# The two passes over the F tiles of a feed-forward layer, in the other order: six tiles first, eight second

## The chip, the cores and the metric

The kernel runs on one core of a Trainium2 chip. Its time is the device time of one execution in microseconds (us), the median over runs. One further execution was recorded by the hardware profiler, and all rows below are from that one. TensorE (PE in the rows) multiplies matrices and writes PSUM; PEld is its loading of weights, which overlaps the multiplying. VectorE (DVE), ScalarE (ACT) and GpSimd (POOL) do the elementwise work; SyncE (SP) issues the DMA transfers, one after the other in the order of its queue. Each engine works through its own queue in order, and a semaphore holds it where an operand isn't there yet.

## The reference

```python
xn = _layernorm(x)                          # x: 8192 tokens of 448
s  = irfft(mlp(rfft(xn)))                   # Fourier transform over the tokens, a two-layer
                                            # complex MLP in 4 blocks of 112, soft threshold
g  = silu((gelu(xn @ w_gate) * (xn @ w_up)) @ w_down)      # D = 448, F = 1792
out = x + s * g
```

All is float32; the kernel splits each operand into a high and a low fp16 half and adds three products.

## The kernel before, in words

The tokens go in 16 chunks of 512, and F in 14 tiles of 128. The weights of all 14 F tiles do not fit at once, so the feed-forward layer (`ffn`) goes over the F tiles in two passes, `PF`: pass 0 over tiles 0 to 7, pass 1 over tiles 8 to 13. Pass 0 leaves its part of the down product in DRAM (`prt`); pass 1 reads it back (`pt`), adds its own and goes on with silu.

Within a pass a chunk (`chunk`) handles its F tiles in pairs. One pair is a `unit`: seven products of half-size operands (`a1` to `a7`, `product`) in the manner of Strassen and Winograd, on combined weights (`wt[f]`, slots 8 to 15, made by `gu_comb`) and on transposed combinations of the tokens, which come by two transposing DMA loads per chunk: `xta` (products 1, 5, 6, 7) and `xtb` (2, 3, 4). Both rings have one buffer: the load of the next chunk's `xta` can start when the last unit of a chunk has done its products on `xta`, that of `xtb` after the unit's last product `a4`. After the units come the down products (`down`), four groups of tokens by three matmuls for each F tile; they cover these loads.

Chunks 0 and 1 of pass 0 go another way (`plain`): 22 matmuls of 512 columns for each F tile, on plain transposes, because the combinations aren't made yet. At their end the down products of both chunks are done together. The down inputs of the second chunk (its h, fp16 halves) and its transposed tokens lie in slots of `wt` that the combined weights of tiles 2 to 7 need later, so `gu_comb` waits on the events `spare`, set tile by tile while the second chunk's down product runs.

While pass 0 runs, phase 1 goes on beside it: `chunk1(c)` for c = 2 to 17 loads the tokens of chunk c (16 and 17 are chunks 0 and 1 again, for pass 1), normalises them, writes the combinations to DRAM (`xts`), and does the first stage of the Fourier transform (`stage1`: 12 matmuls, results `ysb`). Beside that the weights of pass 1's tiles are prepared (`gu_block(b, 1)`), written to DRAM (`wsp`, `dsp`) and fetched at the end of pass 0 (`far_pair`, `far_down`). Phase 2 (`zero`, `group`: the middle of the transform and its MLP) and phase 3 (`tiles3`: the inverse transform and the output) go beside the rest of the feed-forward layer.

The order of instructions on all engines is fixed when the program is built. A planner (`Pace`) keeps an estimated clock for each engine and lets the tasks issue in the order of their estimated times; some have due times written by hand: `chunk1(c)` starts at `T1 + (c - 2) * DT`, with T1 = 84 and DT = 40. On the chip these due times do nothing but decide the order. PSUM has two banks for each of `bx`, `by`, `bd`, `bf`; the two `by` banks are freed by VectorE's additions `u<-by,u` and `v<-by,v`.

Of the kernel before, what the change touches and what calls it, by code (L numbers as in the profile page):

```python
# [26 lines left out]
BLK = ((0, 1), (1, 1)) + tuple((f, 2) for f in range(2, 14, 2))  # L27
NBK = len(BLK)

PF = ((0, 8), (8, 6))  # L30
PB = ((0, 5), (5, 8))
K1, K2 = 256, 192


# [286 lines left out]
def afno_geglu_kernel(ctx, tc, x, gu, wd, mlp, b1, b2, c_m, c_mt, c_small, out):  # L321
# [22 lines left out]
    def ring(pool, shape, dt, name, bufs):  # L344
        return Ring(pace, pool, shape, dt, name, bufs)
# [28 lines left out]
    mhalf = cp.tile([128, CH], F32, name="mhalf")  # L374


    wt = [cp.tile([128, 2, 16, 128], F16, name=f"wt{f}") for f in range(PF[0][1])]
    dw = [cp.tile([128, PF[0][1], D], F16, name=f"dw{i}") for i in range(2)]
    ms = cp.tile([128, 32], F32, name="ms")
    cB = [fb[:, 0:1], fb[:, 1:2]]  # L380
    cF = ms[:, 24:25]
# [22 lines left out]
    EV = {}  # L404

    def ev(*key):
        return EV.setdefault(key, Event())
# [20 lines left out]
    WO = ring(wp, [128, 2, 14, 128], F16, "wo", 1)  # L428
    XTA = ring(fp, [128, XA // 128, 256], F16, "xta", 1)
    XTB = ring(fp, [128, (XW - XA) // 128, 256], F16, "xtb", 1)  # L430
    HT = ring(fp, [128, PF[0][1], 2, 512], F16, "h", 1)
    U1 = ring(fp, [128, 512], F32, "u1", 2)
    U5 = ring(fp, [128, 512], F32, "u5", 1)
    V1 = ring(fp, [128, 512], F32, "v1", 1)
# [153 lines left out]
            if c + 1 < NG + PL:  # L588
                yield ev("phase", c)

    T1, DT = 84.0, 40.0


    def gu_loads(fs, again):
# [83 lines left out]
    def gu_comb(f, t, d):  # L678

        c = yield from CB.get()  # L680
        S.activation(t[:, 4:9], t[:, 4:9], AF.Copy, scale=scale(f, 2))
        yield
        b22 = t[:, 2:10:7]
        for o, p, q in ((c[:, 0:2], t[:, 0:2], t[:, 4:6]), (c[:, 2:4], b22, c[:, 0:2]), (c[:, 4:6], b22, t[:, 0:2]),
                        (c[:, 6], t[:, 6], c[:, 2]), (c[:, 7], t[:, 7], t[:, 3]), (t[:, 8], t[:, 10], t[:, 8])):
            B.tensor_sub(o, p, q)
            yield
        B.tensor_add(c[:, 7], c[:, 7], t[:, 8])
        yield
        WS.put(t)  # L690
        yield
        if 2 <= f < PF[0][1]:
            yield ev("spare", f - 2 if f < 6 else f)
        S.activation(d[:, 0], c, AF.Copy, scale=scale(f, 0))
        yield
        V.scalar_tensor_tensor(d[:, 1], c, scale(f, 0), d[:, 0], op0=ALU.mult, op1=ALU.subtract)
        CB.put(c)
        yield
        done("comb", f)

    def down_weights(p):
        fp0, nf = PF[p]
        if p == 0:

            parts, rings, kept = [(0, 4), (4, 2), (6, 2)], {0: WO, 4: XTB, 6: CB}, {}
        else:
            parts = [(fp0 + k, min(3, nf - k)) for k in range(0, nf, 3)]

        def load(f, n):
            if p == 0 and f in kept:  # L710
                return kept[f]
            if p == 0:
                t = yield from rings[f].get()
                w = t.rearrange("p s v c -> p (s v c)") if len(t.shape) == 4 else t.rearrange("p a b -> p (a b)")
                w = w if f == 6 else w.bitcast(F32)
            else:
                t = w = yield from WS.get()
            v = w[:, 0:n * D].rearrange("p (t d) -> p t d", t=n)
            if p == 0:
                kept[f] = t, v  # L720
            Q.dma_start(v, wd[128 * f:128 * (f + n), :].rearrange("(t p) d -> p t d", p=128))
            yield
            return t, v

        def most(f, n):
            t, v = yield from load(f, n)
            for i in range(n):
                V.tensor_reduce(dmx[:, f + i:f + i + 1], v[:, i], axis=AXIS.X, op=ALU.max, apply_absolute_value=True)
                yield
            if p == 1:  # L730
                WS.put(t)

        def split(f, n):
            t, v = yield from load(f, n)
            if p == 1:
                do = yield from WO.get()
                dv = do.rearrange("p s v c -> p (s v c)")[:, 0:2 * n * D].rearrange("p (s t c) -> p s t c", s=2, t=n)
            for i in range(n):
                d = [w[:, f + i] for w in dw] if p == 0 else [dv[:, s, i] for s in range(2)]
                sc = fd[:, 2, block(f + i):block(f + i) + 1]  # L740
                S.activation(d[0], v[:, i], AF.Copy, scale=sc)
                yield
                V.scalar_tensor_tensor(d[1], v[:, i], sc, d[0], op0=ALU.mult, op1=ALU.subtract)
                if p == 0:
                    done("dw", f + i)
                yield
            (WS if p == 1 else rings[f]).put(t)
            if p == 1:
                Q.dma_start(dsp[:, :, f - fp0:f - fp0 + n, :], dv)
                WO.put(do)  # L750

        for e in [pace.spawn(most(*q)) for q in parts]:
            yield e
        for b in range(*PB[p]):
            yield ev("scales", b)
        mx, ed, eguv = (fd[:, i] for i in range(3))
        bs, fs = slice(*PB[p]), slice(fp0, fp0 + nf)
        dm = dmx[:, 14 + fp0:14 + fp0 + nf]
        yield from largest(dm, dmx[:, fs], 2.0 ** -30)
        pow2(dm, dm)  # L760
        for b in range(*PB[p]):
            f, n = BLK[b]
            V.tensor_tensor(ed[:, b:b + 1], dmx[:, 14 + f:15 + f], dmx[:, 13 + f + n:14 + f + n], op=ALU.max)
        V.tensor_tensor(eguv[:, bs], fe[:, 0, bs], fe[:, 1, bs], op=ALU.mult)
        V.tensor_tensor(ed[:, bs], eguv[:, bs], ed[:, bs], op=ALU.mult)
        ED, inv = fb[:, 2:3], fb[:, 3:4]
        V.tensor_reduce(ED, ed[:, bs], axis=AXIS.X, op=ALU.max)
        V.reciprocal(inv, ED)
        V.tensor_scalar(eguv[:, bs], eguv[:, bs], inv, 2.0 ** 14, op0=ALU.mult, op1=ALU.mult)
        V.tensor_scalar(cB[p], ED, 2.0 ** -11, None, op0=ALU.mult)  # L770
        yield
        for q in parts:
            e = pace.spawn(split(*q))
            if p == 1:
                yield e
        yield e
# [104 lines left out]
    def xt_load(i, kind, first):  # L881
        yield ev("xts", i)
        R, cols = (XTA, slice(0, XA)) if kind == "a" else (XTB, slice(XA, XW))
        t = EV[f"xt{kind}", first, i] = yield from R.get()
        Q.dma_start_transpose(t, xts[i][:, cols])
        yield
        done("xt", kind, first, i)
# [194 lines left out]
    def ended(p, i, a, b, R):  # L1082
# [33 lines left out]
        Q.dma_start(ov[:, CH * i + a, :], th)  # L1116
        TH.put(th)

    def ffn():
        h = yield from HT.get()  # L1120
        yield ev("xp", 0, 0)

        def spare(n):
            g, k = (2 + n // 2, n % 2)
            return wt[g][:, k, 12:16].rearrange("p k c -> p (k c)")

        def h1(f, s):
            if f < 6:
                return wt[2 + f][:, s, 8:12].rearrange("p k c -> p (k c)")
            return wt[f][:, s, 12:16].rearrange("p k c -> p (k c)")  # L1130

        EV["hT", 0], EV["hT", 1] = (lambda f, s: h[:, f, s]), h1
        EV["xT", 1] = [spare(t) for t in range(7)]
        pace.set(ev("second"))
        nf = PF[0][1]

        n = [0, 0]
        while n[1] < nf:
            if n[0] < nf and (ev("w", n[0]).done or n[1] == n[0] or not all(ev("xp", 1, a).done for a in range(CH))):
                c = 0  # L1140
            else:
                c = 1
            yield from plain(c, n[c])
            yield pe()
            n[c] += 1
            if (c, n[c]) == (0, nf):
                XTA.put(state["xta"])
                pace.spawn(xt_load(PL, "a", 0))
        pace.spawn(xt_load(PL, "b", 0))
        for a in range(CH):  # L1150
            yield from down(0, 0, a, 0, nf, EV["hT", 0])
            yield pe()
        HT.put(h)
        rings = (BD, BD, BX, BX)
        for a in range(CH):
            state["d", a] = yield from rings[a].get()
        for f in range(nf):
            for a in range(CH):
                yield from down(0, 1, a, f, f + 1, h1, rings[a])
            pace.then(lambda f=f: done("spare", f))  # L1160
            yield pe()
        for p in range(2):
            for i in range(NG):
                if p or i >= PL:
                    yield from chunk(p, i)

    def chunk(p, i):
# [33 lines left out]
        XTB.put(xb)  # L1201
        if (p, i) == (0, NG - 1):
            pace.spawn(far_pair(nf // 2 - 1))
        if nxt:
            pace.spawn(xt_load(nxt[1], "b", nxt[0]))
        yield pe()
# [356 lines left out]
    def token(c, a, xs):  # L1563
# [18 lines left out]
        if c == 0:  # L1582
            parts = [(state["plain"][:, :, cols], pt)]
        else:
            yield ev("second")
            parts = [(wt[2 + k][:, 0:2 if k < 3 else 1, 12 + POS[a]], pt[:, 2 * k:min(2 * k + 2, 7)]) for k in range(4)]
        for dst, src in parts:
            if a in (0, 2):
                S.copy(dst, src)
# [126 lines left out]
```

## Time and profile before

| | |
|---|---|
| time, median of 3 runs | 1863.16 us (1861.73 to 1868.89) |
| the profiled execution | 1866.04 us, of which the span of its instructions is 1864.3 us |
| TensorE busy | 1816.7 us, 97% of the span |
| VectorE, ScalarE, GpSimd busy | 67%, 53%, 15% |
| tokens of chunk 0 and 1 (plain), to the last plain matmul | 119.0 us |
| first unit of pass 0 | 159.5 us |
| first matmul of phase 3 | 1500.2 us |

A share of busy time is a mean over the span. TensorE's idle time, and whether it runs at full clock, is to be read by stages.

### The profile page before, as it was taken

What the parts mean: (1) busy time and instruction counts of PE and PEld (TensorE: products, weight loads), DVE (VectorE), ACT (ScalarE), POOL (GpSimd) and SP (SyncE); (2) the same over time, 40 slices, a digit from 0 to 9 for tenths busy, and PEclk for the clock granted to TensorE, in tenths of its full rate; (3) what the DMA queues carried; (4) which work ended last, traced back from release to release, by engine and by line L of the source; (5) the groups of instructions that cost most, each with busy time, mean ns of one, the idle gap of its engine ahead of it and who ended that gap; (6) DMA issues with size and microseconds to landing.
All of it is one profiled execution on the core that took longest, in us unless ns stands there. A gap on an engine that the chain in (4) does not pass through costs nothing. (4 is left out here: it accounts for less than half of the span.)

```text
span 1864.3 us, 35733 instructions
## 1 busy us (share of the span) xinstructions
PE 1816.7 (97%) x14605; PEld 1331.8 (71%) x14605; DVE 1245.0 (67%) x2040; ACT 981.3 (53%) x1683; POOL 287.5 (15%) x365
## 2 busy tenths in 40 slices
PE   6999999999999999999999999999999999999998
PEld 3446677776777766787877877787778767777776
DVE  7867878877766655565656666666676666666556
ACT  4746656656555544464655555565556533333343
POOL 2434345323233123000000000000000000000000
PEclk9999999999999999999999999999999999999999
DMA  6463766674644433405036254333433299989762
GB/s 253 145 172 113 214 194 179 212 223 136 179 107 138 135 91 96 110 11 133 19 119 197 79 133 115 96 83 93 115 81 86 82 352 293 288 271 292 231 177 80
DMA packets 319189, 285.51 MB, mean 153 GB/s; under 512 B 230096, under 2 KB 286544, under 8 KB 319024
## 3 DMA queue, kind: packets, MB, share of 16 engines
q1 hardware_dynamic: 318880, 283.19, 51.6%
q8 instruction: 114, 1.87, 0.4%
q14 instruction: 51, 0.42, 0.1%
q10 hardware_dynamic: 144, 0.03, 0.0%
HBM read 128.44 MB, written 105.58 MB: 126 GB/s over the span
## 5 line engine op out<-in xcount | busy, mean ns | idle before, releaser
L179 PEld LDWEIGHTS <-wt 128*128 128x128 f16 x8582 | 835.0, 98 | 191.1 <-issue 15.1
L179 PE MATMUL bd<-dw,h 128*128 128x448 f16 x2592 | 514.5, 354 | 3.5 <-ACT th L179 1.9
L179 PE MATMUL bx<-xta,wt 128*128 128x256 f16 (+1 forms) x3843 | 475.6, 275 | 9.0 <-ACT u L179 3.9
L179 PEld LDWEIGHTS <-h 128*128 128x128 f16 x2592 | 252.2, 98 | 233.3 <-issue 7.9
L179 PE MATMUL by<-xtb,wt 128*128 128x256 f16 x2080 | 249.5, 273 | 0.8 <-ACT u L179 0.8
L179 PE MATMUL by<-xta,wt 128*128 128x256 f16 (+1 forms) x1347 | 179.2, 283 | 6.5 <-DVE wt L179 3.1
L179 ACT COPY v<-bx 128x512 f32<-128x512 f32 x208 | 121.6, 585 | 98.4 <-PE bx L179 97.6
L179 DVE SCALAR_TENSOR_TENSOR gl<-v,fc,gl 128x512 f32<-128x512 f32 (+1 forms) x118 | 85.9, 737 | 80.4 <-ACT gl L179 80.2
L179 PE MATMUL bx<-xtb,wt 128*128 128x256 f16 x1040 | 130.6, 273 | 0.0
L179 ACT ACTIVATE gl<-bx,fc 128x512 f32<-128x512 f32 (+1 forms) x118 | 73.6, 636 | 88.8 <-PE bx L179 85.5
L179 DVE TENSOR_TENSOR u<-by,u 128x512 f32<-128x512 f32 x104 | 71.5, 687 | 73.1 <-PE by L179 71.8
L179 ACT ACTIVATE u<-u,fc 128x512 f32<-128x512 f32 (+1 forms) x118 | 77.6, 669 | 78.6 <-DVE u L179 78.5
L179 ACT ACTIVATE th<-pt 128x448 f32<-128x448 f32 x64 | 36.8, 576 | 114.1 <-DVE pt L179 109.8
L179 PE MATMUL bf<-z,w1t 112*112 112x512 f16 (+2 forms) x432 | 95.8, 357 | 0.0
L179 ACT ACTIVATE th<-bd,fb 128x448 f32<-128x448 f32 x62 | 38.9, 632 | 106.8 <-PE bd L179 84.0
L179 POOL TENSOR_TENSOR v<-v,u 128x512 f32<-128x512 f32 x20 | 29.5, 1474 | 407.1 <-ACT v L179 358.0
L179 ACT COPY u<-bx 128x512 f32<-128x512 f32 x104 | 60.9, 586 | 59.5 <-PE bx L179 59.2
L179 ACT COPY u<-by 128x512 f32<-128x512 f32 x104 | 60.9, 585 | 55.9 <-PE by L179 46.6
L179 DVE SCALAR_TENSOR_TENSOR u<-v,fc,u 128x512 f32<-128x512 f32 (+1 forms) x118 | 84.7, 727 | 5.9 <-ACT u L179 1.0
L179 DVE TENSOR_TENSOR wn<-h,wn 112x512 f16<-112x512 f32 (+3 forms) x73 | 46.0, 630 | 61.8 <-ACT wn L179 61.1
L179 PE MATMUL bf<-w2t,wn 112*128 112x112 f16 x1536 | 86.3, 213 | 0.0
L179 PEld LDWEIGHTS <-wn 112*128 112x128 f16 x1536 | 81.9, 98 | 4.2
(173 smaller groups left out, 2341.0 us busy)
## 6 DMA issues: line engine op xcount, KB each, us to landing
wst<-in_gu SPq DMA_DIRECT2D x22, 704.0 KB, 6.6
xts<-sx SPq DMA_DIRECT2D x32, 480.0 KB, 2.8
x<-in_x SPq DMA_DIRECT2D x17, 896.0 KB, 6.1
t<-ysb SPq DMA_DIRECT2D x64, 224.0 KB, 3.2
prt<-th SPq DMA_DIRECT2D x64, 224.0 KB, 2.1
pt<-prt SPq DMA_DIRECT2D x64, 224.0 KB, 3.7
u<-t SPq DMA_DIRECT2D x32, 448.0 KB, 5.2
y<-t SPq DMA_DIRECT2D x15, 896.0 KB, 4.9
```

Of the source, the lines that this page charges most:

```text
L179: return self.pace.issue(self.name, kind, out, ins, lambda: fn(out, *args, **kw))
```

## The change

The passes are swapped in size: pass 0 goes over tiles 0 to 5, pass 1 over tiles 6 to 13 (`PF`, and `PB` for the blocks of scales). So `plain` runs over 6 tiles instead of 8, a chunk of pass 0 has 3 units instead of 4, a chunk of pass 1 has 4 instead of 3. Eight instead of six tiles are prepared for pass 1, written to DRAM and fetched. `wt` and `dw` still hold eight tiles; tiles 6 and 7 are empty in pass 0, and hold the second chunk's h (all of `wt[7]`, half of `wt[6]`) and most of its transposed tokens. Only the combinations of tiles 4 and 5 still wait for `spare`, which is now set once, after the last plain matmul. The due times of `chunk1` are 42 apart instead of 40. At the end of pass 0 a fourth pair is fetched.

```diff
-PF = ((0, 8), (8, 6))
-PB = ((0, 5), (5, 8))
+PF = ((0, 6), (6, 8))
+PB = ((0, 4), (4, 8))
...
-    T1, DT = 84.0, 40.0
+    T1, DT = 84.0, 42.0
...
-        if 2 <= f < PF[0][1]:
-            yield ev("spare", f - 2 if f < 6 else f)
+        if 4 <= f < PF[0][1]:
+            yield ev("spare")
...
-            parts, rings, kept = [(0, 4), (4, 2), (6, 2)], {0: WO, 4: XTB, 6: CB}, {}
+            parts, rings, kept = [(0, 4), (4, 2)], {0: WO, 4: XTB}, {}
...
+    XT1 = ((6, 0), (6, 1), (4, 3), (5, 3))
...
-        def spare(n):
-            g, k = (2 + n // 2, n % 2)
-            return wt[g][:, k, 12:16].rearrange("p k c -> p (k c)")
+        def spare(g, k, s):
+            return wt[g][:, s, 4 * k:4 * k + 4].rearrange("p k c -> p (k c)")
...
-            if f < 6:
-                return wt[2 + f][:, s, 8:12].rearrange("p k c -> p (k c)")
-            return wt[f][:, s, 12:16].rearrange("p k c -> p (k c)")
+            return spare(6, 2 + f, s) if f < 2 else spare(7, f - 2, s)
...
+        pace.then(lambda: done("spare"))
         pace.spawn(xt_load(PL, "b", 0))
...
-            pace.then(lambda f=f: done("spare", f))
...
         if (p, i) == (0, NG - 1):
             pace.spawn(far_pair(nf // 2 - 1))
+            pace.spawn(far_pair(nf // 2))
```

How the order moves shows best in SP's queue. The first place is in pass 0, around the fourth load of `xta`, which is that of chunk 5. Before, it stands behind the last writes of `xts` for chunk 7 (the five rows ahead of it):

```order
L179 DMA t<-ysb 64x1792 x2
L179 DMA xts<-sx 128x1920
L179 DMA xts<-xs 128x2x256
L179 DMA xts<-xs 128x2x192
L179 DMA xts<-xs 128x2x64
L179 DMA xts<-xs 128x2x128
L179 DMA_TRANSPOSE xta<-xts 128x16x256
L179 DMA t<-ysb 64x1792 x2
L179 DMA_TRANSPOSE xtb<-xts 128x9x256
L179 DMA prt<-th 128x448 x2
```

In the changed kernel the same load, the fourth, stands behind the last writes for chunk 5 itself:

```order
L179 DMA xts<-sx 128x1920
L179 DMA xts<-xs 128x2x256
L179 DMA xts<-xs 128x2x192
L179 DMA xts<-xs 128x2x64
L179 DMA xts<-xs 128x2x128
L179 DMA t<-ysb 64x1792 x2
L179 DMA_TRANSPOSE xta<-xts 128x16x256
L179 DMA_TRANSPOSE xtb<-xts 128x9x256
L179 DMA wsp<-wo 128x3584
L179 DMA prt<-th 128x448 x3
```

So the making of the combinations was two chunks ahead of their use by then, and is now just ahead of it; the writes and the stage-1 results (`t<-ysb`) of the same chunk stand directly ahead of its load.

The second place is in SP's queue too, at the end of pass 0, where the weights of pass 1 are fetched. Before (`wt_76` to `wt_83` are `wt[0]` to `wt[7]`), the load of `xta` for pass 1's first chunk stands behind all six tiles:

```order
L179 DMA wt_78<-wsp 128x2x1792
L179 DMA wt_79<-wsp 128x2x1792
L179 DMA wt_80<-wsp 128x2x1792
L179 DMA wt_81<-wsp 128x2x1792
L179 DMA_TRANSPOSE xta<-xts 128x16x256
L179 DMA y<-t 128x4x896
L179 DMA_TRANSPOSE xtb<-xts 128x9x256
```

In the changed kernel:

```order
L179 DMA wt_78<-wsp 128x2x1792
L179 DMA wt_79<-wsp 128x2x1792
L179 DMA_TRANSPOSE xta<-xts 128x16x256
L179 DMA wt_80<-wsp 128x2x1792
L179 DMA wt_81<-wsp 128x2x1792
L179 DMA wt_82<-wsp 128x2x1792
L179 DMA wt_83<-wsp 128x2x1792
L179 DMA_TRANSPOSE xtb<-xts 128x9x256
L179 DMA prt<-th 128x448 x2
L179 DMA dw_84<-dsp 128x3584
```

Four tiles now stand between `xta` and `xtb`.

## Rows read from the trace of the kernel before

**Rows 1.** The page, busy time of each engine over the span.

```profile
PE 1816.7 (97%) x14605; PEld 1331.8 (71%) x14605; DVE 1245.0 (67%) x2040; ACT 981.3 (53%) x1683; POOL 287.5 (15%) x365
```

**Rows 2.** Busy time by stages: stretch, its length, engines' busy us, PEclk, DMA share, GB/s.

```profile
25.00:119.00 94.00, 90.93 (x450) 42.86 (x448) 75.21 (x152) 59.30 (x111) 40.17 (x50) 0.98 0.54 172
119.00:159.50 40.50, 38.75 (x205) 19.96 (x204) 26.23 (x53) 18.63 (x29) 7.40 (x12) 1.00 0.54 163
159.50:740.00 580.50, 568.11 (x4310) 421.11 (x4309) 416.49 (x713) 327.36 (x594) 209.38 (x274) 0.99 0.55 157
740.00:1440.00 700.00, 696.58 (x6462) 539.75 (x6460) 441.86 (x668) 403.47 (x660) 15.51 (x12) 1.00 0.36 97
1440.00:1864.00 424.00, 412.54 (x3138) 302.90 (x3136) 268.77 (x414) 165.69 (x279) 9.72 (x7) 0.99 0.74 228
```

**Rows 3.** Timeline of PE, two halves of a plain tile: start, us, instruction.

```profile
71.62 2.54 PE L179 MATMUL bx<-xta,wt 128*128 128x512 f16 x11
74.00 2.54 PE L179 MATMUL by<-xta,wt 128*128 128x512 f16 x11
```

**Rows 4.** Timeline of PE, third and fourth unit of chunk 3 in pass 0.

```profile
242.20 2.35 PE L179 MATMUL by<-xtb,wt 128*128 128x256 f16 x20
...
248.31 1.25 PE L179 MATMUL bx<-xtb,wt 128*128 128x256 f16 x10
249.40 1.47 PE L179 MATMUL bx<-xta,wt 128*128 128x256 f16 x12
250.71 2.35 PE L179 MATMUL by<-xtb,wt 128*128 128x256 f16 x20
```

**Rows 5.** Timeline of PE, down products of chunk 0, and stage 1 behind them.

```profile
119.00 18.32 PE L179 MATMUL bd<-dw,h 128*128 128x448 f16 x96
137.16 1.30 PE L179 MATMUL bf<-xs,m 128*128 128x448 f16 x6
```

**Rows 6.** Waits of PE from 159.5 to 740 us: total, times, longest.

```profile
PE bf L179 <- DVE xs L179: 0.3, 1, 0.3
```

**Rows 7.** Stretches of 20 us, then 24 down matmuls after a wait and elsewhere.

```profile
160.00:180.00 20.00, 18.37 (x167) 16.00 (x165) 17.95 (x28) 12.25 (x23) 14.77 (x20) 1.00 0.25 84
720.00:740.00 20.00, 17.07 (x113) 10.49 (x111) 1.09 (x3) 4.99 (x10) 0.00 (x0) 0.91 0.44 124
...
728.70 0.69 PE L179 MATMUL bf<-sm,y 128*112 128x130 f16 x6 [2.93 <-issue]
729.19 6.25 PE L179 MATMUL bd<-dw,h 128*128 128x448 f16 x24
...
1020.88 4.70 PE L179 MATMUL bd<-dw,h 128*128 128x448 f16 x24
```

**Rows 8.** DMA issues (size, median us to landing), and SP's issue times in ns.

```profile
wt<-wsp SPq DMA_DIRECT2D x6, 896.0 KB, 5.9
xta<-xts SPq DMA_TRANSPOSE x30, 7.0
xtb<-xts SPq DMA_TRANSPOSE x30, 5.2
...
L179 SPq DMA_TRANSPOSE xta<-xts x30: 3917/4257/8448, 113.3 to 1798.0; - x30
```

**Rows 9.** Timeline of DVE: first and one later step of chunk1 for chunk 3.

```profile
122.03 0.62 DVE L179 BATCH_NORM_STATS2 st<-x 128x6 f32<-128x448 f32 x1
...
129.78 1.09 DVE L179 TENSOR_TENSOR xs<-x,xs 128x896 f16<-128x896 f32 x1 [0.46 <-ACT xs L179]
```

**Rows 10.** Timeline of PE, a chunk that waits for its transposed load.

```profile
1505.95 1.64 PE L179 MATMUL bx<-xta,wt 128*128 128x256 f16 x12 [2.43 <-DMA xta<-xts]
```

**Rows 11.** Timeline of PE and DVE at the end of the kernel.

```profile
1845.76 11.51 PE L179 MATMUL bd<-dw,h 128*128 128x448 f16 x60
1848.18 0.69 DVE L179 TENSOR_TENSOR h<-gl,h 128x512 f16<-128x512 f32 x1 [0.68 <-ACT h L179]
1858.15 0.68 DVE L179 SCALAR_TENSOR_TENSOR pt<-bd,fb,pt 128x448 f32<-128x448 f32 x1 [0.50 <-DMA pt<-prt]
```

More of the change, by code (lines that the diff above doesn't have):

```diff
@@ L374, in afno_geglu_kernel @@
     mhalf = cp.tile([128, CH], F32, name="mhalf")
-    wt = [cp.tile([128, 2, 16, 128], F16, name=f"wt{f}") for f in range(PF[0][1])]
-    dw = [cp.tile([128, PF[0][1], D], F16, name=f"dw{i}") for i in range(2)]
+    wt = [cp.tile([128, 2, 16, 128], F16, name=f"wt{f}") for f in range(PF[1][1])]
+    dw = [cp.tile([128, PF[1][1], D], F16, name=f"dw{i}") for i in range(2)]
     ms = cp.tile([128, 32], F32, name="ms")
@@ L430, in afno_geglu_kernel @@
     XTB = ring(fp, [128, (XW - XA) // 128, 256], F16, "xtb", 1)
-    HT = ring(fp, [128, PF[0][1], 2, 512], F16, "h", 1)
+    HT = ring(fp, [128, PF[1][1], 2, 512], F16, "h", 1)
     U1 = ring(fp, [128, 512], F32, "u1", 2)
@@ L714, in load @@
                 w = t.rearrange("p s v c -> p (s v c)") if len(t.shape) == 4 else t.rearrange("p a b -> p (a b)")
-                w = w if f == 6 else w.bitcast(F32)
+                w = w.bitcast(F32)
             else:
@@ L1121, in ffn @@
         yield ev("xp", 0, 0)
-        def spare(n):
-            g, k = (2 + n // 2, n % 2)
-            return wt[g][:, k, 12:16].rearrange("p k c -> p (k c)")
+        def spare(g, k, s):
+            return wt[g][:, s, 4 * k:4 * k + 4].rearrange("p k c -> p (k c)")
         def h1(f, s):
-            if f < 6:
-                return wt[2 + f][:, s, 8:12].rearrange("p k c -> p (k c)")
-            return wt[f][:, s, 12:16].rearrange("p k c -> p (k c)")
+            return spare(6, 2 + f, s) if f < 2 else spare(7, f - 2, s)
         EV["hT", 0], EV["hT", 1] = (lambda f, s: h[:, f, s]), h1
-        EV["xT", 1] = [spare(t) for t in range(7)]
+        EV["xT", 1] = [spare(g, k, s) for g, k in XT1 for s in range(2)][0:7]
         pace.set(ev("second"))
@@ L1585, in token @@
             yield ev("second")
-            parts = [(wt[2 + k][:, 0:2 if k < 3 else 1, 12 + POS[a]], pt[:, 2 * k:min(2 * k + 2, 7)]) for k in range(4)]
+            parts = [(wt[g][:, 0:2 if n < 3 else 1, 4 * k + POS[a]], pt[:, 2 * n:min(2 * n + 2, 7)])
+                     for n, (g, k) in enumerate(XT1)]
         for dst, src in parts:
```

## The prediction, made before the changed kernel ran

> **What bounds the kernel now.** The page's busy times come first [rows 1]: TensorE works through 97% of the span, and no other engine passes 67%. A change can gain in two ways only, by fewer matmul columns or by less idle time on TensorE. So the second view is busy time by stages [rows 2]. Its first two columns are the length of a stretch and TensorE's busy time in it, and their difference is idle time: 94.00 - 90.93 = 3.1 us in the plain stage, 1.8 us to the first unit, 12.4 us in phase 1, 3.4 us in phase 2, 11.5 us in the last stretch. In the last the final matmul ends at 1845.76 + 11.51 = 1857.3 [rows 11], so 6.7 us of it are the tail behind TensorE and 4.8 us lie inside. Idle time that another order could win back is then 1.8 + 12.4 + 3.4 + 4.8 = 22.4 us, 1.2% of the span. VectorE is busy for 416.49 of 580.50 us in phase 1, 72% [rows 2]: a chain that runs through it can be late, but its throughput is no bound. The waits of TensorE in phase 1 are many and short; the longest, 2.9 us, is that before the first matmul of phase 2 [rows 6, 7].
>
> **The plain chunks.** Half of a plain tile is 11 matmuls, and one begins 74.00 - 71.62 = 2.38 us after the other [rows 3]: 4.76 us for a tile and a chunk. A unit does two tiles: from the products by<-xtb of the third unit to those of the fourth it is 250.71 - 242.20 = 8.51 us [rows 4], 4.26 us for a tile. The change takes two tiles from each of two plain chunks and gives them to pass 1: 4 x (4.76 - 4.26) = 2.0 us fewer. The down products keep their number. Each tile's 12 matmuls for a chunk stand in pass 0 or in pass 1, and cost 137.16 - 119.00 = 18.16 us for 96, or 0.189 us each [rows 5]. That is the sure gain: -2.0.
>
> The event `spare` costs nothing in my sum. Combined weights of tiles 2 and 3 no longer wait, those of 4 and 5 wait for the end of the plain matmuls, some 30 us of down products ahead of their first use; these cover it. Without the cover it would be one wait, between the shortest and the longest of the waits in [rows 6, 10], 0.3 to 2.4 us.
>
> **Pass 0.** A chunk there has now 3 x 8.51 = 25.5 us of units, 72 x 0.189 = 13.6 us of down products and 12 stage-1 matmuls (six take at most 1.30 us [rows 5], so 2.6): 41.7 us instead of 54.8. `chunk1` keeps its work per chunk, so its lead is gone: in SP's queue the transposed load now follows the writes of its own chunk, where it had two chunks in hand. Whether TensorE waits is a question of two chains.
>
> The first is DMA. `xta` comes free when a chunk's last unit has done its products on it; then 13.6 us of down products and the products a4 (249.40 - 248.31 = 1.1 us [rows 4]) are left, 14.7 us, against a landing of 7.0 us [rows 8]. Its own issue takes SP 4.3 us, then `xtb` lands in 5.2 us: 9.5 us after `xta` came free, and it is needed later still. Both fit, with 7 us in hand. The pass of 6 tiles before had the same 13.6 us to cover its loads, and waited for one once [rows 10].
>
> The second is VectorE. In the new order the statistics of the next chunk stand behind the last h of the chunk before. The last h ends 1848.87 - 1845.76 = 3.1 us after the last a4 [rows 11]; a4 ends 60 x 0.189 = 11.3 us ahead of the next chunk, so h ends 8.2 us ahead. From the first statistics to the end of the first xs took 130.87 - 122.03 = 8.8 us where little else stood between them [rows 9]. So xs is ready 0.6 us into the chunk. Its stage-1 matmuls stand later than that in TensorE's queue: in the second unit at first, at the chunk's beginning in the last chunks, where the statistics stand ahead of the last h and gain the 3 us that they need. It fits, but with only a few us to spare, and while weights are prepared their steps stand in between. I take no change in phase 1's 12.4 us: 14 shorter chunks instead of 10.6 longer ones, the same work of VectorE, and a chain that now falls mostly into the down products, where TensorE needs VectorE least. Bounds: 9.5 us less, if all but the 2.9 us at phase 2's start goes [rows 6, 7]; 31.6 us more, if 13 chunks wait as that of [rows 10] does.
>
> **The end of pass 0.** Four tiles stand between `xta` and `xtb`. SP issues `xta` 14.7 us ahead of pass 1's first chunk and is done 10.4 us ahead; then come 4 x 896 KB, 3.67 MB, and `xtb`, which is needed after three groups of 12 products on `xta` (250.71 - 249.40 = 1.3 us each [rows 4]), 3.9 us into the chunk: 14.3 us in all. One tile lands in 5.9 us [rows 8]. If four share the way at the 228 GB/s of the busiest stretch [rows 2] they take 16 us and `xtb` lands some 5 us after, 7 us late; if they overlap fully, it isn't late. I take 1.5 us, nearer to no wait, since the load of `xtb` need not stand behind all of their bytes. Before, phase 2's matmuls stretched this place and hid it.
>
> **The last stretch.** A chunk of pass 1 grows by a unit and 24 down matmuls, 8.51 + 24 x 0.189 = 13.0 us, so its loads come less often; the wait of 2.4 us in the crowded start of phase 3 [rows 10] may go or stay: -1.2, bounds 0 and -2.4. At the very end VectorE's step on the last group came 1858.15 - 1857.27 = 0.9 us after the last matmul, since its pt waited for a buffer [rows 11]. Groups now are 24 instead of 18 matmuls, 1.1 us more each, so it is there in time: -0.8.
>
> **The sum.** -2.0 + 0 + 1.5 - 1.2 - 0.8 = -2.5 us. Against the profiled execution (span 1864.3, time 1866.0) this gives 1863.5; that execution was 2.9 us above the median of the runs, so the median to expect is 1860.7, or 1861.
>
> **Rivals.** *Faster: the waits go.* In the new order loads, statistics and stage 1 stand in the same place in each chunk, and pass 1 asks for fewer loads per us. For it: most waits of phase 1 are VectorE's or ScalarE's, which drift against the units now. If half of the 22.4 us goes, the gain is 2.8 + 11.2 = 14.0, so 1849. It decides from 6.5 us of the 22.4. Against it: the steps that collide are all still there.
>
> *Slower: the lost lead is felt in every chunk.* TensorE comes to stage 1, or to a product behind VectorE's additions, before VectorE is there, in each of the 13 chunks from 3 to 15. The price of one such wait lies between 0.3 us [rows 6] and 2.4 us [rows 10], 4 to 32 us in all; in the middle, 18, the time is 1879. It decides from 0.9 us per chunk (12 us, of which the gains eat 2.5). For it: less than a microsecond in hand on VectorE in the stage in which weights are prepared, where 20 us hold 17.95 us of its work [rows 7]. Against it: in that very stretch TensorE lost 1.6 us only, and a chunk that is late leaves time to the others to catch up.
>
> A wait can cost more than itself. After the 2.93 us before phase 2 the granted clock of the stretch is 0.91, and 24 down matmuls took 6.25 us where others took 4.70: 1.55 us at the lower of the clock's two levels, 1.2 instead of 2.4 GHz; the stretch with a loss of 1.6 us kept 1.00 [rows 7]. The Trainium skill (TensorE: Matmul & The Clock Gate, section "HAM oscillation — how this bites in real kernels") tells of a kernel that waited once for each tile of its work and fell to the lower clock after every one of the waits. By that rule the 13 waits of the slower rival would each cost 1.55 us on top, 20 us, and its time would be 1899; I give this 0.06 of the slower rival's chance. The trace agrees for the long wait and not for the short ones.
>
> *No change in the waits, but a longer end of pass 0*: the 7 us bound there, 1866. It stays within what can be told.
>
> **How the numbers follow.** A measurement of this kernel tells about 0.5%, 9.3 us, from no change: faster is below 1853.8, slower above 1872.5. Forecast 0.43; the long end of pass 0 0.07, nearly all of it within; faster rival 0.27; slower rival 0.23. So 0.27 faster, 0.49 same, 0.24 slower. The forecast's own range is 1855 to 1871. For 8 in 10 it reaches to the middle of the faster rival's gain and a little beyond, 1846, and to a wait of 1.9 us per chunk in the slower one (1861 + 25), 1886.
>
> **What would show it.** The plain stage should end near 97 us (119.0 less 4 x 4.76 and the stage 1 of chunk 2, which moves behind it), the first unit come near 129 (159.5 less the same 19.0, 48 x 0.189 of down products and the stage 1 of chunk 3); chunks of pass 0 should follow each other in about 42 to 43 us; TensorE's busy time should fall by some 2 us and no more. Right is the chain if its idle time between the first unit and pass 1 is 10 to 16 us. Wrong it is if stage-1 matmuls wait for xs, or products for by, in most chunks; if TensorE waits for `xta` anywhere in pass 0; or if the clock falls below 0.99 in that stretch.

## The result, and the profile after

The changed kernel takes 1869.69 us (median of 20 runs, 1865.42 to 1876.14), the kernel before 1862.26 us beside it (20 runs, 1859.04 to 1868.89). The ratio is 1.0039, with a 95% interval of 1.003 to 1.0048: slower by 7.4 us, where 2 us less had been forecast. The profiled execution of the changed kernel took 1868.96 us (span 1867.2). That of the kernel before lay 3.8 us above its own median, so the two profiles show only 2.9 us of the 7.4 between them. One execution of a later kernel (due times 40) went at a granted clock of 0.85 from start to end and took 2110 us; no row below is from it.

The page's busy times, to be laid beside [rows 1]:

```profile
PE 1813.6 (97%) x14673; PEld 1339.2 (72%) x14673; DVE 1254.3 (67%) x2072; ACT 980.6 (53%) x1687; POOL 256.4 (14%) x339
```

TensorE's busy time fell by 3.1 us. Its idle time rose from 1864.3 - 1816.7 = 47.6 to 1867.2 - 1813.6 = 53.6 us. Where, the busy times by stages tell (columns as in [rows 2]; the stages are the plain chunks with 3.5 us of the down products that follow, the rest of those down products, pass 0, the first part of pass 1, the rest):

```profile
25.00:97.30 72.30, 69.82 (x360) 33.79 (x360) 62.59 (x135) 47.94 (x87) 27.22 (x34) 1.00 0.41 139
97.30:127.60 30.30, 26.20 (x140) 13.44 (x139) 18.95 (x34) 12.11 (x21) 11.01 (x17) 0.97 0.74 195
127.60:740.00 612.40, 592.67 (x4469) 438.32 (x4469) 440.55 (x776) 349.55 (x640) 184.82 (x256) 0.99 0.64 184
740.00:1440.00 700.00, 695.24 (x6383) 536.84 (x6381) 446.50 (x671) 390.79 (x639) 21.07 (x19) 1.00 0.34 92
1440.00:1867.20 427.20, 419.91 (x3275) 311.46 (x3273) 269.27 (x417) 173.38 (x290) 6.96 (x5) 1.00 0.66 209
```

Length less busy time: 2.5 us idle in the plain stage (3.1 before), 4.1 in the next (1.8), 19.7 in pass 0 (12.4), 4.8 in the next (3.4), 7.3 in the last (11.5). So the last stretch won 4 us, and the stretch from 97.3 us to pass 1 lost them and more. What TensorE waits for there, by groups (what waits, for what: us in total, times, longest), 97.3 to 765 us, to be laid beside [rows 6]:

```profile
PE bx L179 <- ACT u L179: 10.4, 5, 4.8
PE bf L179 <- DVE fx L179: 4.5, 2, 2.7
PE bx L179 <- ACT th L179: 4.1, 1, 4.1
PE by L179 <- ACT u L179: 2.8, 2, 1.7
PE bf L179 <- DVE ysb L179: 2.6, 2, 1.7
...
PE bf L179 <- DVE xs L179: 0.6, 1, 0.6
```

No wait for `xta` or `xtb` is among them, and one of 0.6 us for `xs`: the two chains that the prediction had examined held. ScalarE's copies of products (`u`, `v`) and its `th` came late instead. ScalarE's own waits have one group that is far larger in the changed kernel, 97.3 to 765 us (first row), than in the kernel before, 119 to 740 us (second row):

```profile
ACT th L179 <- DMA prt<-th: 48.0, 13, 9.2
...
ACT th L179 <- DMA prt<-th: 8.4, 4, 4.4
```

`th` is the result of a down product on its way to DRAM: ScalarE writes it from PSUM, the store `prt<-th` frees it, and the ring has two buffers. A chunk of pass 0 makes four of them during its down products. The first two come 1.1 us apart (`th` at 163.72 and 164.86), and each of the others after 18 more matmuls, 3.4 us by the 0.189 us of [rows 5]; before, those were 24 matmuls or 4.5 us. What that does shows first at the first unit. The timeline of SP, ScalarE and TensorE:

```profile
120.78 2.95 SPq L179 DMA_TRANSPOSE xtb<-xts  x1
121.87 1.20 ACT L179 ACTIVATE th<-bd,fb 128x448 f32<-128x448 f32 x2 [9.10 <-issue]
124.19 0.82 SPq L179 DMA_DIRECT2D prt<-th  x2
126.90 1.25 ACT L179 ACTIVATE th<-bx,fb 128x448 f32<-128x448 f32 x2 [3.83 <-DMA prt<-th]
127.59 2.72 PE L179 MATMUL bx<-xta,wt 128*128 128x256 f16 x12 [4.10 <-ACT th L179]
130.10 2.71 PE L179 MATMUL by<-xta,wt 128*128 128x256 f16 x12
132.65 1.48 PE L179 MATMUL bx<-xta,wt 128*128 128x256 f16 x12
```

Two th are written at 121.87, and their stores stand behind `xtb` in SP's queue. The third th waits for the first store to land, 3.83 us. It would empty a `bx` bank, and the first unit needs that bank: TensorE stands still for 4.10 us. Its next 24 matmuls then run at half speed, 2.7 us for twelve where twelve take 1.48 later. In the kernel before, the same two results waited 0.46 us for their store and the unit 1.76 us:

```profile
158.83 1.21 ACT L179 ACTIVATE th<-bx,fb 128x448 f32<-128x448 f32 x2 [0.46 <-DMA prt<-th]
...
159.52 1.47 PE L179 MATMUL bx<-xta,wt 128*128 128x256 f16 x12 [1.76 <-ACT th L179]
```

The same wait stands at the other end of pass 0, where `xtb` follows four loads of 896 KB:

```profile
733.40 9.88 SPq L179 DMA_TRANSPOSE xtb<-xts  x1
743.38 1.00 SPq L179 DMA_DIRECT2D prt<-th  x2
...
746.99 0.63 ACT L179 ACTIVATE th<-bd,fb 128x448 f32<-128x448 f32 x1 [3.66 <-DMA prt<-th]
747.52 0.58 ACT L179 COPY u<-bx 128x512 f32<-128x512 f32 x1
...
748.15 2.72 PE L179 MATMUL bx<-xta,wt 128*128 128x256 f16 x12 [4.76 <-ACT u L179]
```

SP is held by the issue of `xtb` for 9.88 us, so the stores of two results that were written by 734.6 are issued from 743.4 on, the next `th` waits, and behind it in ScalarE's queue the copy `u<-bx` that frees the bank for pass 1's first chunk.

### The profile page after: what moved, and what is told of

Same layout as the page of the kernel before. It is cut to its first block, busy times and chain, and to the rows that moved or that the text cites. A ratio compares the mean times of both kernels' runs of the same rounds, so it can differ in the third digit from the quotient of the medians.

```text
span 1867.2 us, 35881 instructions
## 1 busy us (share of the span) xinstructions
PE 1813.6 (97%) x14673; PEld 1339.2 (72%) x14673; DVE 1254.3 (67%) x2072; ACT 980.6 (53%) x1687; POOL 256.4 (14%) x339
## 4 chain that ended last, share of the span: by engine, by line
PE 64%; DMA 1%; SPq 1%; DVE 0%; ACT 0%; issue 0%; POOL 0%; DVEq 0%; ACTq 0%; POOLq 0%
PE bx L179 19%; PE bd L179 17%; PE bf L179 15%; PE by L179 13%; SPq L179 1%; DMA prt<-th 1%; DMA pt<-prt 1%; POOL sf L179 0%; ACT sx L179 0%; ACT u L179 0%; DVE pt L179 0%; DVE th L179 0%; DVE x L179 0%; DVE sx L179 0%; DVE u L179 0%
## 5 line engine op out<-in xcount | busy, mean ns | idle before, releaser
L179 PE MATMUL bx<-xta,wt 128*128 128x256 f16 (+1 forms) x3893 | 481.2, 275 | 16.4 <-ACT u L179 11.5
L179 PE MATMUL by<-xtb,wt 128*128 128x256 f16 x2120 | 258.4, 274 | 2.8 <-ACT u L179 2.8
L179 PE MATMUL by<-xta,wt 128*128 128x256 f16 (+1 forms) x1349 | 174.6, 279 | 4.9 <-DVE wt L179 3.1
L179 DVE SCALAR_TENSOR_TENSOR pt<-bd,fb,pt 128x448 f32<-128x448 f32 x64 | 43.6, 682 | 85.3 <-PE bd L179 59.6
L179 DVE SCALAR_TENSOR_TENSOR u<-v,fc,u 128x512 f32<-128x512 f32 (+1 forms) x120 | 88.6, 748 | 6.3 <-ACT u L179 0.8
L179 ACT CAST h<-gl 128x512 f16<-128x512 f32 x106 | 65.7, 620 | 37.3 <-DVE gl L179 37.3
L179 DVE TENSOR_TENSOR v<-by,v 128x512 f32<-128x512 f32 x106 | 72.5, 684 | 12.7 <-PE by L179 10.6
```

The costliest lines, as they stand in the source:

```text
L179: return self.pace.issue(self.name, kind, out, ins, lambda: fn(out, *args, **kw))
```

## The experiments

The theory was then: the ring of `th` is too short for the shorter chunk, because its stores stand behind the transposed loads in SP's queue. The main rival was the lead of `chunk1`, lost as the prediction had feared: VectorE or the loads come late in each chunk. All edits but those of due times and of the early fetch leave TensorE's and VectorE's order of instructions exactly as it was. Differences "against the changed kernel" are worked out as (ratio - 1.0039) x 1862 us, each ratio being against the kernel before on the same chip; by the intervals they are sure to some 3 us.

| kernel | us | ratio, interval | against the changed kernel |
|---|---|---|---|
| changed, 4 th buffers | 1866.17 | 1.0017, 1.0005 to 1.0029 | -4.1 |
| changed, 4 th buffers except in the last chunk | 1859.16 | 0.998, 0.9971 to 0.999 | -11.0 |
| changed, tiles 6 and 7 fetched early | 1864.71 | 1.0009, 0.9996 to 1.0021 | -5.6 |
| changed, weights from ScalarE's queue | 1865.55 | 1.0011, 1.0 to 1.0022 | -5.2 |
| changed, 4 th buffers and early fetch | 1855.63 | 0.9957, 0.9944 to 0.997 | -15.3 |
| changed, all three | 1848.99 | 0.9931, 0.9918 to 0.9943 | -20.1 |
| changed, th stores from ScalarE's queue | 1876.77 | 1.0083, 1.0069 to 1.0096 | +8.2 |
| changed, th stores from GpSimd's queue | 1884.22 | 1.0115, 1.01 to 1.0131 | +14.2 |
| changed, due times 40 apart | 1886.55 | 1.0122, 1.0105 to 1.0138 | +15.5 |
| changed, due times 44 apart | 1922.03 | 1.0328, 1.0314 to 1.0342 | +53.8 |
| before, 4 th buffers | 1862.48 | 0.9999, 0.9987 to 1.0011 | |
| before, weights from ScalarE's queue | 1862.05 | 0.9989, 0.9977 to 1.0 | |
| before, due times 42 apart | 1859.13 | 0.9984, 0.9973 to 0.9995 | |
| before, all of these three | 1858.15 | 0.9965, 0.9954 to 0.9975 | |

**Four buffers for th.** The ring of `pt` has the same shape and isn't used in pass 0 before its last chunk, so two of every four results go there.

```diff
-            th = yield from TH.get()
+            th = yield from TH.get(tag="th" if a < 2 else "pt")
```

> The changed kernel with four buffers for th in pass 0 instead of two (the two buffers of pt, which lie unused in pass 0, take every other pair); the order of instructions on every engine is the same. Store theory (ScalarE waits at th because the stores prt<-th stand behind xta and xtb in SP's queue, and the copy u<-bx behind th comes late for TensorE): ScalarE's waits of th for prt<-th from 129 to 760 us fall from 43.1 us to under 10, TensorE's waits of bx for u from 10.4 to under 5 us, the 4.1 us before the first unit go, and the time is 1860 to 1865 us (1869.7 without). Lost-lead theory (VectorE's chain for each chunk comes late): TensorE's idle time stays within 3 us, 1867 to 1872 us.

Measured: 1866.17 us, 3.5 us less by the medians and just above the store theory's range. The wait at the first unit went, and ScalarE waited no more for a store in the chunks before the last (44.3 us from 97.3 to 735 us without the edit); pass 1's first matmul came at 728.08 instead of 740.61 us. But then 11 us were lost at one place, which the timeline of ScalarE and TensorE shows:

```profile
745.02 0.63 ACT L179 ACTIVATE pt<-bd,fb 128x448 f32<-128x448 f32 x1 [11.21 <-DMA prt<-pt]
...
746.18 2.29 PE L179 MATMUL by<-xtb,wt 128*128 128x256 f16 x10 [11.38 <-ACT u L179]
```

This is a flaw of the edit: in the last chunk of pass 0 the `pt` buffers are already wanted for pass 1's first loads, and the last result got the buffer whose store stood behind the whole fetch. The control, the same edit in the kernel before:

> The same four buffers in the kernel before, also with the order unchanged. Store theory: there a chunk lasts 54.8 us for the same four stores and no wait of TensorE ends with them, so the time stays within 2 us of 1862. If it falls by 4 us or more, the buffers of th are a cost of their own that the change did not bring. Lost-lead theory: within 2 us too.

Measured: 1862.48 us against 1862.77, no change. The buffers are no cost of the kernel before.

**The same without the flaw**, with two buffers in the last chunk:

```diff
-            th = yield from TH.get()
+            th = yield from TH.get(tag="th" if a < 2 or i == NG - 1 else "pt")
```

> Four buffers for th again, but not in pass 0's last chunk, where the two of pt are loaded for pass 1 already; order as in the changed kernel. In the run with four buffers for all chunks pass 1 began 12.5 us earlier, and then one th waited 11.2 us for a buffer that the load of pt had taken. Store theory: what was gained ahead of pass 1 is kept, and the switch waits some 5 us as in the changed kernel without four buffers: 1858 to 1863 us. If the time gained ahead of pass 1 is always given back at the switch (the transposed load or the weights of pass 1 are late whatever comes before): 1865 to 1868 us.

Measured: 1859.16 us, 10.5 us less than the changed kernel by the medians and 0.2% below the kernel before. TensorE's timeline has the first unit 3.06 us earlier than after the change, at full speed, and the wait at the switch unchanged:

```profile
124.53 1.48 PE L179 MATMUL bx<-xta,wt 128*128 128x256 f16 x12 [0.20 <-ACT pt L179]
...
739.57 2.41 PE L179 MATMUL bx<-xta,wt 128*128 128x256 f16 x12 [4.84 <-ACT u L179]
```

The first down product behind that unit comes at 151.26 instead of 156.75, so the one wait of 4.1 us cost 5.5 us with its slow matmuls. Pass 1 began 8.7 us earlier (731.95 against 740.61); the remaining 3.2 us are small waits in the chunks between. The gain is larger than the 7.4 us that the change lost, so the rival, which expected none, isn't needed as a cause.

**Tiles 6 and 7 fetched early.** The fourth pair is fetched at the start of pass 0's last chunk, since those two tiles of `wt` were free long before.

```diff
+        if (p, i) == (0, NG - 1):
+            pace.spawn(far_pair(nf // 2))
...
-            pace.spawn(far_pair(nf // 2))
```

> The changed kernel with the weights of tiles 6 and 7 of pass 1 fetched at the start of pass 0's last chunk instead of behind its last a4, so that only two tiles stand between xta and xtb; everything ahead of that chunk is unchanged. Store theory: the wait of 4.8 us at 748 us, in the first chunk of pass 1, comes from xtb and the stores behind it being issued behind four tiles; it falls to under 2 us, and the time is 1865 to 1867 us. If the wait there has to do with VectorE or phase 2: it stays, 1868 to 1871 us.

Measured: 1864.71 us, 5.0 us less by the medians. That is 0.3 us below the store theory's range. SP's issue of `xtb` took 6.56 instead of 9.88 us, and TensorE's wait at the switch became

```profile
741.73 1.47 PE L179 MATMUL bx<-xta,wt 128*128 128x256 f16 x12 [1.01 <-ACT u L179]
```

**Both:**

> Both edits: four buffers for th in all but the last chunk of pass 0, and tiles 6 and 7 fetched at the start of that chunk. Store theory: the two gains add, -5 from the fetch and -6 to -10 from the buffers, 1855 to 1859 us, below the kernel before at 1862. If both hide the same wait: 1861 to 1865 us.

Measured: 1855.63 us; the gains add (-11.0 and -5.6 give -16.6, measured -15.3), so they are different waits.

**The store's place in the queue, or its landing.** Two kernels keep two buffers and the order, and issue the stores elsewhere: right behind `th` on ScalarE's queue, or on GpSimd's.

```diff
-            Q.dma_start(prt[i][:, a * D:(a + 1) * D], th)
+            pace.issue("SP", "dma_start", dst, [src], lambda: nc.gpsimd.dma_start(dst, src))
```

(`nc.scalar` in the other; the planner's books go on counting it as SP's, which keeps the order.)

> The changed kernel with two buffers for th, but its stores prt<-th issued from GpSimd's queue instead of SP's, in the same order. Store theory (the place in SP's queue holds the buffers): ScalarE's waits of th for the store fall from 46.9 us to under 20, the 4.1 us before the first unit go, 1858 to 1865 us. If two buffers are too few wherever the store is issued: the waits stay above 35 us, 1867 to 1872 us. Unknown is what the issue costs GpSimd, whose sf and x steps stand in the same queue.

> The changed kernel with two buffers for th, and its stores prt<-th issued from ScalarE's own queue right behind each th instead of SP's; the order on every engine is the same. From GpSimd's queue they stood among GpSimd's steps and the result said little. If the place in SP's queue holds the buffers: ScalarE's waits of th for the store fall from 46.9 us to under 25, 1858 to 1866 us. If two buffers are too few even for a store that is issued at once, since it takes some 3 us to land and four results end within 12 us: the waits stay above 35 us, 1867 to 1872 us. At the first unit, where two results come at once, the wait of 4 us stays in either case.

Measured: 1884.22 us from GpSimd and 1876.77 from ScalarE, both slower than the changed kernel and outside both ranges given for them. ScalarE's waits for the store fell from 48.0 to 40.0 and 27.1 us; 27.1 lies between the two expectations. TensorE's time did not fall, and the first unit waited 3.70 and 3.88 us still. A store that ScalarE issues at once, in the timeline of that run:

```profile
212.89 1.14 ACT L179 ACTIVATE th<-bd,fb 128x448 f32<-128x448 f32 x2
213.54 0.85 ACTq L1090 DMA_DIRECT2D prt<-th  x2
217.33 0.64 ACT L179 ACTIVATE th<-bd,fb 128x448 f32<-128x448 f32 x1 [3.30 <-DMA prt<-th]
```

ScalarE waits 3.30 us for a buffer even so, `xtb` being on its way at the same time. So another queue is no mend: with two buffers the third result waited in all three kernels, and only more buffers took the waits away. How much of the 48.0 us is the place in SP's queue stays open, since moving the stores brought costs of its own. Why these two kernels came out 8 and 14 us above the changed one isn't settled. On GpSimd the trace shows the store waiting for `th` in front of that engine's own steps for the next chunk:

```profile
260.99 0.61 POOL L1090 DMA_DIRECT2D prt<-th  x1 [4.63 <-ACT th L179]
```

That explains a part by argument only.

**The lead.** The due times of `chunk1`, the one number of the change that was chosen freely:

```diff
-    T1, DT = 84.0, 42.0
+    T1, DT = 84.0, 40.0
```

> The changed kernel with the due times of chunk1 40 us apart as before, instead of 42. Lost-lead theory: the preparation of a chunk gets ahead again by 2 us per chunk in the planned order, waits for fx, xs and u become fewer, 1862 to 1866 us. Store theory: the stores stand behind the transposed loads as they did, ScalarE waits over 25 us for them, and the time stays at 1867 to 1873 us.

> Due times 40 us apart once more, since the profile of that run had a granted clock of 0.85 from start to end and can't be laid beside the others. If the order with 40 costs 17 us by itself: 1880 to 1890 us again, with idle time of TensorE in pass 0 some 15 us above the changed kernel's, or work of phase 1 that is pushed into other stages. If it was the clock: 1866 to 1873 us.

> The changed kernel with due times 44 us apart. Chunks follow each other in 43.8 us there. If a later preparation is felt in each chunk (lost lead): the products and stage 1 wait for xs and fx, 1875 to 1890 us. If the lead doesn't matter and the waits come from the stores and loads in SP's queue: 1864 to 1874 us.

Measured: 1887.12 us with 40 (1885.29 without the execution of 2110 us), 1886.55 us in a second run of it, 1922.03 us with 44. Neither theory had 1887 or 1922 in its range, and 40 is no gain as the rival had it; that 40 costs its 17 us again, as the second run's text says for the order by itself, came true. With 40 the waits for `fx` shrink to 1.3 us, but the preparation now stands ahead of the chunk's own h, and the down products wait for h, in the groups of TensorE's waits from 97.3 to 765 us (second run):

```profile
PE bd L179 <- DVE h L179: 5.2, 5, 1.8
...
PE bd L179 <- ACT h L179: 4.0, 3, 3.4
```

That is a part of the cost. In all, TensorE's idle time rose by 10.7 us over the changed kernel's, to 64.3, and its busy time by 9.0 us for the same number of matmuls, at a granted clock of 0.992 instead of 0.994.

With 44 the writes of `xts` come too late for their load, and the same view begins with a group that the prediction had named among the signs of its chain being wrong:

```profile
PE bx L179 <- DMA xta<-xts: 14.8, 5, 4.7
PE bx L179 <- ACT u L179: 14.3, 6, 3.6
```

Over the whole run TensorE waited 27.9 us for `xta`, 13.1 of them at 798 us, ahead of pass 1. In the changed kernel the lead fits at 42, and 2 us per chunk to either side break it. The rival describes the kernel with 44, not the one that was predicted. In the kernel before:

> The kernel before with the due times of chunk1 42 us apart instead of 40, the one part of the change that can be made alone. If due times 40 apart suit only a chunk of 55 us and any order near it does as well: 1860 to 1866 us. If each due time gives another order, whose collisions differ by ten us and more, as 40 did in the changed kernel (1887): outside 1855 to 1870 us.

Measured: 1859.13 us, 3.0 us below 1862.17 on the same chip and just under the first range. There two us of due time move little, and to the better. That its chunk of 54.8 us leaves room is a likely reason that no run isolates.

**The loads of weights.** TensorE's second group, 4.5 us for `fx` (the scales of pass 1's tiles), goes back to SP's queue too: the weights are issued behind `xta` and `xtb`, VectorE waits for them, and TensorE for VectorE. The timeline of the changed kernel:

```profile
161.15 3.03 SPq L179 DMA_TRANSPOSE xtb<-xts  x1
164.22 1.05 SPq L179 DMA_DIRECT2D wst<-in_gu  x2
169.56 1.22 DVE L179 TENSOR_REDUCE fm<-wst 128x2 f32<-128x1024 f32 x1 [6.33 <-DMA wst<-in_gu]
172.83 1.22 DVE L179 TENSOR_REDUCE fm<-wst 128x2 f32<-128x1024 f32 x1 [2.05 <-DMA wst<-in_gu]
174.31 0.38 PE L179 MATMUL bf<-identf,fx 128*2 128x128 f32 x2 [2.67 <-DVE fx L179]
```

The edit issues them from ScalarE's queue, at the same place of the order, in the best version, in the changed kernel alone and in the kernel before:

```diff
-            Q.dma_start(t, gu[f])
+            eng = nc.scalar if f >= 6 and not again else nc.sync
+            pace.issue("SP", "dma_start", t, [gu[f]], lambda: eng.dma_start(t, gu[f]))
```

> The best version so far (four buffers for th, tiles 6 and 7 fetched early), with the weights of pass 1's tiles (wst<-in_gu) loaded from ScalarE's queue instead of SP's, where they stand directly behind xta and xtb. If the waits of TensorE for fx (5.8 us, two times) come from that place: VectorE's reduction of wst no longer waits 6 us for the load, the fx waits fall to under 3 us, 1850 to 1854 us (1855.6 without). If VectorE is late for fx by its own work: the waits stay, 1854 to 1857 us.

> The changed kernel with one edit, the weights of pass 1's tiles loaded from ScalarE's queue; two buffers for th, tiles 6 and 7 fetched late, the same order. If the loads behind xta and xtb are a cost of the new order by themselves: 1862 to 1866 us (1869.7 without). If the 6.6 us that this gave in the best version came only together with the other two edits: 1867 to 1871 us.

> The kernel before with the same edit. No wait of TensorE for fx stands there (0 of 4), so if the cost came with the change: 1860 to 1864 us, no change. If these loads cost the kernel before as well: 1854 to 1858 us.

Measured: 1848.99 us (6.6 less than without, 1 us below its range), 1865.55 us (4.1 less by the medians), and 1862.05 us in the kernel before, where the interval ends at no change. So most of this cost came with the change. How it was saved was expected only in part. One wait for `fx` of 2.5 us stayed in the best version (3.2 without the edit), since the second of the two loads was still read 10.7 us after the issue began; the other (2.5 us) went. A part of the gain is the clock: behind its waits of 3.21 and 2.54 us the version without the edit had a granted clock of 0.83 from 160 to 180 us and of 0.91 from 340 to 360, and with the edit both are 1.00. The rest lies in small pieces along pass 0. The Trainium skill (Trainium Kernel Development and Optimization, section "Key Constraints") states that transfers issued from several engines run on the same DMA engines, and that another queue saves the issue time alone. The two loads agree with it: with their issue begun at 157.88 on ScalarE's queue, VectorE read them at 163.39 and 168.60; in the version without the edit it began at 158.01 on SP's, and they were read at 163.31 and 167.35.

**The kernel before with all that can be taken over:**

> The kernel before with all that can be taken over: four buffers for th, the weights from ScalarE's queue, due times 42 apart (1859.1 alone). If the mends serve only what the change brought: 1856 to 1861 us, some 8 to 11 us above the changed kernel with its three mends (1849). If they are gains of any order: 1847 to 1853 us.

Measured: 1858.15 us, ratio 0.9965, against 0.9931 for the changed kernel with its three mends. The intervals don't touch. With the same care the new order of the passes is the better one, by 0.34% or 6 us; as it was changed, it was the worse.

## Why the prediction was right or wrong

**The columns** (-2.0): TensorE's busy time fell by 3.1 us, but it holds slow matmuls in both kernels and doesn't measure this term. The plain stage ended at 93.8 us, not near 97: the down products begin there.

```profile
93.81 6.97 PE L179 MATMUL bd<-dw,h 128*128 128x448 f16 x36
```

The 3 us beyond the forecast are no columns. The kernel before had a granted clock of 0.98 in its plain stage [rows 2], the changed kernel 1.00. Behind a wait of 1.64 us, which the changed kernel doesn't have, 11 plain matmuls of the kernel before took 4.24 us where others take 2.54 [rows 3]:

```profile
56.08 4.24 PE L179 MATMUL by<-xta,wt 128*128 128x512 f16 x11
```

The first unit came at 127.6 (129 forecast). That this fits is luck: an early plain stage and a wait of 4.10 us that nobody had forecast cancel. The price of a tile is neither confirmed nor contradicted.

**`spare` costs nothing**: no wait of TensorE for the combined weights is among the groups. But just there, at the first unit, stands the wait for `th`, 5.5 us with its slow matmuls where 1.76 stood before. The prediction's price for an uncovered wait (0.3 to 2.4 us) was too small for it.

**Pass 0, "I take no change in phase 1's 12.4 us"** is the step that failed. Between the first unit and pass 1 TensorE was idle for 19.7 us, where the prediction had called 10 to 16 the sign that its chain was right. From 97.3 us to the end of the wait at the switch (748.15) it was idle for 650.85 - 622.27 = 28.6 us, against 1.8 + 12.4 = 14.2 before, from 119 to 740 us, over the same phase 1. Chunks follow each other in 43.8 us (forecast 42 to 43), by the first and the last of their fourteen first down products:

```profile
156.75 2.43 PE L179 MATMUL bd<-dw,h 128*128 128x448 f16 x12
...
725.90 2.43 PE L179 MATMUL bd<-dw,h 128*128 128x448 f16 x12
```

The working behind the step was right in what it looked at: `xta` was never late, xs once by 0.6 us. It asked of two chains only, loads and VectorE. The third, from the down product through `th` to its store, has the same four results in a chunk of 42 us instead of 55, the last two of them 3.4 us apart instead of 4.5. The prediction counted its stores nowhere, though in the piece of order shown for the end of pass 0 `prt<-th` stands directly behind `xtb`. Four buffers give back 11.0 us, more than the 7.4 that the change lost, and nothing in the kernel before. With them the changed kernel lies 0.2% or 3.7 us below the kernel before; the sum had said 2.5.

**The end of pass 0** (+1.5, bound 7): the wait is 4.8 us, inside the bound, and the early fetch gives 5.0 to 5.6 back. The way was another one: what TensorE waited for is what stood behind the issue of `xtb`, the stores of `th`. The lateness of `xtb` itself, which the term was about, is hidden under that wait. The DMA view from 726 to 750 us gives its time from issue to landing, and the timeline the start of pass 1:

```profile
xtb<-xts SPq DMA_TRANSPOSE x1, 12.6
...
740.61 1.47 PE L179 MATMUL bx<-xta,wt 128*128 128x256 f16 x12
```

Issued at 733.40, it landed at 746.0. TensorE would have wanted it three groups of 1.3 us after 740.61, at 744.5. So it was 1.5 us late, as the prediction took it; with four buffers in all chunks TensorE did wait for it, for 0.2 us.

**The last stretch** (-1.2) and **the tail** (-0.8): the wait of [rows 10] went, two waits of 0.9 and 0.3 us are left in the whole last stretch, and VectorE's step on the last group follows the last matmul (1846.11 + 14.92 = 1861.03) within 0.04 us instead of 0.9:

```profile
1861.07 0.68 DVE L179 SCALAR_TENSOR_TENSOR pt<-bd,fb,pt 128x448 f32<-128x448 f32 x1 [1.82 <-PE bd L179]
```

Idle time of the last stretch fell from 11.5 to 7.3 us, more than the 2.0 forecast.

**The rivals.** The slower one had the right side and the wrong place: not a wait in each of 13 chunks for VectorE or `xta`, but a ring of buffers that costs 5.5 us once, 4.8 us at the switch, and some 3 us in the chunks between. Its own signs show with due times 44 apart. The faster one gave 1849, the time of the version with the three mends; the agreement is luck, since it wanted the waits to go by the new order alone. The measured 1869.69 lies inside the forecast's range of 1855 to 1871 by the width of that range: the sum pointed the other way.

**The clock.** The rule of the Trainium skill (TensorE: Matmul & The Clock Gate, section "HAM oscillation — how this bites in real kernels"), that a wait can throw TensorE to the lower clock, agrees with the long waits here and not with each of the shorter ones. In the windows of the changed kernel the granted clock is 0.83 around the wait of 4.10 us, and 1.00 in the stretch with the wait of 2.67 us:

```profile
120.00:140.00 20.00, 15.90 (x111) 11.76 (x110) 5.02 (x9) 8.13 (x15) 2.52 (x3) 0.83 0.59 164
...
160.00:200.00 40.00, 36.35 (x278) 26.81 (x276) 28.19 (x47) 21.40 (x41) 19.13 (x23) 1.00 0.56 165
```

Of the two levels, 1.2 and 2.4 GHz, the lower stood behind three waits of this stage, 4.10 us at the first unit, 4.76 us at the switch, and one of 2.23 us (at 442.64, with a granted clock of 0.91 from 440 to 460 us). The one of 2.67 us kept the full clock, so the length of the wait alone doesn't tell.

## What to carry to other kernels

When a loop gets shorter, list every ring whose use per turn stays the same, stores out of the loop among them, and set the time from the write of a result to the landing of its store against the time in which as many results come as there are buffers. Here two buffers, held for 5 us and more, met two results 1.1 us apart and a third 3.4 us later. A transfer that looks harmless can hold an engine two steps on: SP's queue held the store, the store the buffer, the buffer ScalarE, and ScalarE's next copy the PSUM bank that TensorE wanted. A reordered kernel should be compared only after its transfers have been placed for the new order: this change was worth +7 us as made. With one ring lengthened and two kinds of transfers moved it was worth -13 us against the kernel before, and -6 against the kernel before with what of this can be taken over.

## What the runs showed of the hardware that was not expected

The store of 224 KB landed more slowly in the kernel in which the transposed loads are more frequent; that they are the reason isn't shown. The DMA view from 97 to 740 us gives its median time from issue to landing, in the kernel before

```profile
prt<-th SPq DMA_DIRECT2D x48, 224.0 KB, 2.1
```

and in the changed kernel

```profile
prt<-th SPq DMA_DIRECT2D x60, 224.0 KB, 3.3
```

And the issue of a transposed load on SP is not a fixed cost. It took 2.95 us for `xtb` at the first unit and 2.2 to 5.3 in the other chunks of pass 0 before the last, but 6.56 behind two loads of 896 KB and 9.88 behind four, and all that SP has to issue after it waits that long.
